# Attention and two gated layers on one core: the written order goes on through three units of the second block, with two places for values

## The chip, the cores and the metric

One core of one Trainium2 chip runs the whole program. The metric is the device time of one execution in microseconds (us), as the median of several runs. PE is the matrix engine, ACT the scalar engine, DVE the vector engine, POOL the GpSimd engine and SP the engine whose queue issues the transfers between DRAM and SBUF here.

## The reference

```python
# attention: chunks of 32 queries see 8 memory keys, 16 keys to the left, the chunk, 8 to the right
scores = scale * np.matmul(q_c, k_full.transpose(0, 1, 3, 2))
scores = scores - np.max(scores, axis=-1, keepdims=True)
a = np.exp(scores)
a = a / (np.sum(a, axis=-1, keepdims=True) + 1e-09)
out[:, :, c_start:c_end] = np.matmul(a, v_full)
...
x = out.transpose(0, 2, 1, 3).reshape(B * S, H * D)      # 3072 tokens x 512
h = x @ w_in                                             # 512 x 2048, float64
x = (h * (1.0 / (1.0 + np.exp(-1.702 * h)))) @ w_out     # 2048 x 512
g = x @ w_gate                                           # 512 x 1536
return (g * (1.0 / (1.0 + np.exp(-g))) * (x @ w_val) @ w_out2)
```

q, k and v are float32 of 4 batches, 8 heads, 768 positions, 64 wide; the weights of the layers come from the host as 64-bit floats. All arithmetic is done on the core.

## The kernel before

**Tiles.** The 3072 tokens are 24 *groups* of 128 (attention works on these) and 6 *blocks* of 512 (the layers work on these; block 0 is made of groups 0 to 3). The first layer has 8 *units* of 256 hidden columns. A unit of an ordinary block is a fast product: seven products of six matmuls of 256 columns (`product`, L430) into the banks `ps_a` and `ps_b`, with copies on ACT and additions on DVE between them, then curve, gate, cast and remainder for each half, then four *down chunks* of six matmuls (`down`, L558), one for each 128 output columns, which add up in the banks y0 to y3. Each operand of a product is held as a rounded part and a remainder, so a "split" is a cast on ACT and a subtraction on POOL or DVE.

**Token sums.** The seven operands of a block's products are made once for a block from its 128x4x512 tile `xf` (class `Tokens`, L381): `sum(k)` forms four differences, two of them in place in `xf`, `split_hi` and `split_lo` make the rounded parts and remainders.

**Weights.** A unit needs four tiles of 64-bit words (`raw`, 512 KB each, loaded by `load_raw`, L258; for the first layer those of the input weights come in two transfers of 64 partitions). A tile is turned into float32 by one ACT and two DVE instructions (L279, L287, L292), then POOL forms sums and the splits follow.

**Attention of a group.** Keys (`kbd`) and queries are loaded, `ps_s` gets the scores, DVE and ACT make the weights, four PE transposes turn them (`ps_t`), ACT copies them into `ebd`, the value product (`ps_o`, or `ps_v` in the opening) reads `ebd` and `vm`, ACT copies the result into `xf` and SP stores it to DRAM (`xd`). There is one place for values (`vm`) and two for turned weights (`ebd`).

**What sets the order.** Every engine executes in the order in which the program issues. The *opening* is written out by hand: the string `OPENING` (L796) is a list of names, and each name issues one step on its engine. It holds the attention of groups 0 to 7, the plain products of units 0 and 1 for block 0 (`plain_up`, L519; 48 matmuls of 512 columns), the first unit's down chunks, the weights of units 0 and 1, and the token sums of block 1. Behind it runs a loop (L865) over the blocks and units: it issues a unit (`unit`, L448), puts down chunks of earlier units between its products, takes one step of the next block's attention at fixed places (`PLACES`, L855), and lets `pace` (L820) make weights ahead. The first entries of the loop's list are block 0 with units 0 and 1 and blocks 1 to 5 with units 0 to 3. In the opening SP's transfers stand in the written order too.

Of the kernel before, what the change touches and what calls it, by code (L numbers as in the profile page):

```python
# [57 lines left out]
def tile_attention_moe_moe(  # L58
# [40 lines left out]
    vm = apool.tile([P, HP, 4, D], F32, name="vm")  # L99
    ebd = [apool.tile([P, HP, 4, 2, CH], F32, name=f"ebd{i}") for i in range(2)]  # L100
# [12 lines left out]
    def load_kv(n, g):  # L113
        if n == "v":
            nc.sync.dma_start(out=vm, in_=vg[g])
# [42 lines left out]

    def keep_e(g, ps, engs):
        for e, copy in enumerate(engs):  # L160
            r = slice(64 * e, 64 * e + 64)
            copy(ebd[g % 2][r, :, :, e, :], ps[r].rearrange("p a (c q) -> p a c q", c=4))  # L162

    def values(g, ps, v):
        ps = ps.rearrange("p (a q) -> p a q", a=KC)
        for a in range(0, HP, 2):
            for c in range(4):
                for j in range(2):
# [3 lines left out]
                        ebd[g % 2][:, a + j, c].rearrange("p e q -> p (e q)"),  # L172
# [17 lines left out]
    def st_scores(g):  # L190
        ps = bank("ps_s").rearrange("p (h k) -> p h k", h=H)
        q = qt.pop(g)
        for hp in range(HP):
            for c in range(4):
# [3 lines left out]
                )  # L198
        if g + 1 < NG:
# [74 lines left out]
    nraw, bits = [len(AT)], {}  # L274
# [80 lines left out]
    ready = {(1, u) for u in range(PLAIN)}  # L355

    def all_weights():
        for ph in (1, 2):
            for u in range(PLAIN if ph == 1 else 0, UNITS[ph]):
# [4 lines left out]
    need, made = [next(weights)], [20 * PLAIN]  # L364
# [16 lines left out]
    class Tokens:  # L381


        def __init__(self, src, engs):
            n = BLK // 2
            self.b11, self.b12 = src[:, 0:2, :n], src[:, 0:2, n:]
# [4 lines left out]
        def sum(self, k):  # L391
# [5 lines left out]
            elif k == 1:  # L397
                eng.tensor_sub(self.b12, self.b12, self.b11)
# [3 lines left out]
            else:  # L402
                eng.tensor_sub(self.b11, self.b21, self.t2)  # L403

# [153 lines left out]
    def down(ph, b, u, first, last, gs, base, dst, d, scale, passes=PASSES):  # L558
# [16 lines left out]
        if ends:  # L575
            del acc[d]
            if base is not None:
                t = base[d]
                nc.vector.scalar_tensor_tensor(t, y, scale, t, op0=ALU.mult, op1=ALU.add)
            else:  # L580
                t = opool.tile([P, 512], F32, tag="o", name="o")
                if d % 2 == 0:
                    nc.scalar.activation(t, y, AF.Copy, scale=scale)
                else:
                    nc.vector.tensor_scalar_mul(t, y, scale)
# [388 lines left out]
```

## Time and profile before

| | us |
|---|---|
| median of 3 runs | 1205.7 |
| lowest and highest | 1204.4, 1206.23 |
| the profiled execution | 1204.81 |
| its span | 1203.0 |
| PE busy | 1155.2 (96%) |
| DVE, ACT, POOL busy | 649.2, 566.7, 352.5 |

The span runs from the first to the last instruction that the profiler records; the profiled execution's own time is 1.8 us longer. Busy times of different engines lie beside each other, so they do not add up. A busy PE may still run at a lower clock, which a line of the page shows by the slice.

### The profile page before, as it was taken

What the parts mean: (1) busy time and instruction counts of PE and PEld (TensorE: products, weight loads), DVE (VectorE), ACT (ScalarE), POOL (GpSimd) and SP (SyncE); (2) the same over time, 40 slices, a digit from 0 to 9 for tenths busy, and PEclk for the clock granted to TensorE, in tenths of its full rate; (3) what the DMA queues carried; (4) which work ended last, traced back from release to release, by engine and by line L of the source; (5) the groups of instructions that cost most, each with busy time, mean ns of one, the idle gap of its engine ahead of it and who ended that gap; (6) DMA issues with size and microseconds to landing.
All of it is one profiled execution on the core that took longest, in us unless ns stands there. A gap on an engine that the chain in (4) does not pass through costs nothing.

```text
span 1203.0 us, 22302 instructions
## 1 busy us (share of the span) xinstructions
PE 1155.2 (96%) x8908; PEld 1042.7 (87%) x8908; DVE 649.2 (54%) x1117; ACT 566.7 (47%) x1185; POOL 352.5 (29%) x321
## 2 busy tenths in 40 slices
PE   4868899999999999999999999999999999999998
PEld 3757788888889999898998989999998989999997
DVE  6666665575674444443456564444556454454553
ACT  4655555454565544543465553342455443343342
POOL 2653312020455331320245433120255521020110
PEclk9888999999999999999999999999999999999999
DMA  9957363633434324223222331110225120320302
GB/s 309 301 161 196 120 177 104 170 106 114 141 123 124 105 89 140 85 74 106 96 97 88 123 123 36 71 55 17 88 76 168 56 97 10 106 80 27 106 23 84
DMA packets 62920, 131.47 MB, mean 109 GB/s; under 512 B 5728, under 2 KB 26208, under 8 KB 60512
## 3 DMA queue, kind: packets, MB, share of 16 engines
q1 hardware_dynamic: 62816, 130.05, 34.5%
q8 instruction: 70, 1.15, 0.4%
q14 instruction: 34, 0.28, 0.1%
HBM read 98.57 MB, written 31.46 MB: 108 GB/s over the span
## 4 chain that ended last, share of the span: by engine, by line
PE 85%; DMA 4%; DVE 4%; ACT 3%; issue 2%; POOL 1%; SPq 0%; DVEq 0%; ACTq 0%; POOLq 0%
PE y L568 35%; PE ps_a L433 26%; PE ps_c L433 12%; PE ps_b L433 8%; DMA raw<-in_wr 1%; DMA vm<-in_vg 1%; PE ps_o L169 1%; PE ps_s L196 1%; PE ps_u L529 1%; DMA xd<-xf 1%; DMA w<-in_kg 1%; PE ps_t L156 1%; ACT ebd L162 0%; DVE gs L548 0%; DVE b L419 0%
## 5 line engine op out<-in xcount | busy, mean ns | idle before, releaser
L433 PEld LDWEIGHTS ps_a<-b,w 128*128 128x128 f32 x2832 | 385.3, 190 | 50.6 <-ACT p L466 11.4
L433 PE MATMUL ps_a<-b,w 128*128 128x256 f32 x2832 | 398.6, 283 | 16.2 <-ACT p L466 10.1
L568 PE MATMUL y<-gs,w 128*128 128x512 f32 x1152 | 300.4, 396 | 1.0 <-DVE gs L548 0.8
L568 PE MATMUL y<-w,gs 128*128 128x512 f32 x864 | 247.8, 395 | 0.6 <-DVE gs L548 0.5
L568 PEld LDWEIGHTS y<-gs,w 128*128 128x128 f32 x1152 | 204.6, 190 | 37.1 <-DVE gs L548 2.3
L433 PE MATMUL ps_c<-b,w 128*128 128x256 f32 x1224 | 179.1, 282 | 0.0
L433 PEld LDWEIGHTS ps_c<-b,w 128*128 128x128 f32 x1224 | 167.1, 190 | 8.8
L568 PEld LDWEIGHTS y<-w,gs 128*128 128x128 f32 x864 | 144.2, 190 | 14.5 <-DVE gs L548 1.7
L249 POOL TENSOR_TENSOR w<-wf,w 128x512 fp32r<-128x512 f32 (+1 forms) x68 | 78.0, 1148 | 227.3 <-ACT w L246 215.2
L433 PE MATMUL ps_b<-b,w 128*128 128x256 f32 x900 | 135.4, 287 | 1.0 <-DVE e L131 0.5
L433 PEld LDWEIGHTS ps_b<-b,w 128*128 128x128 f32 x900 | 120.7, 193 | 5.8 <-issue 2.1
L536 ACT ACTIVATE g<-ps_b 128x512 f32<-128x512 f32 x72 | 43.0, 598 | 166.0 <-DVE ps_b L491 166.0
L419 DVE TENSOR_TENSOR b<-xl,b 128x512 fp32r<-128x512 f32 x72 | 64.5, 895 | 80.5 <-ACT b L415 80.3
L485 DVE TENSOR_TENSOR ps_a<-m,ps_a 128x256 f32<-128x256 f32 x118 | 50.2, 425 | 105.4 <-PE ps_a L433 99.4
L475 ACT COPY u<-ps_a 128x256 f32<-128x256 f32 x118 | 44.0, 373 | 109.1 <-PE ps_a L433 108.8
L403 POOL TENSOR_TENSOR xl<-xl,t 128x512 f32<-128x512 f32 x18 | 23.3, 1293 | 231.0 <-DVE t L401 229.8
L548 DVE TENSOR_TENSOR gs<-ps_a,gs 128x512 fp32r<-128x512 f32 x118 | 80.9, 686 | 10.4 <-ACT gs L544 10.1
L470 DVE TENSOR_TENSOR ps_b<-p,ps_b 128x256 f32<-128x256 f32 x118 | 50.4, 427 | 60.6 <-PE ps_b L433 55.2
L544 ACT CAST gs<-ps_a 128x512 fp32r<-128x512 f32 x118 | 69.8, 591 | 25.1 <-DVE ps_a L514 15.7
L514 DVE TENSOR_TENSOR ps_a<-g,ps_a 128x512 f32<-128x512 f32 x72 | 50.0, 694 | 46.0 <-PE ps_a L433 45.5
L466 ACT COPY p<-ps_a 128x256 f32<-128x256 f32 x118 | 44.0, 373 | 58.4 <-PE ps_a L433 54.2
L491 DVE TENSOR_TENSOR ps_b<-u,ps_c 128x256 f32<-128x256 f32 x102 | 43.6, 427 | 50.0 <-PE ps_c L433 49.7
(112 smaller groups left out, 1182.4 us busy)
## 6 DMA issues: line engine op xcount, KB each, us to landing
raw<-in_wr SPq DMA_DIRECT2D x49, 512.0 KB, 3.4
xl<-yd SPq DMA_DIRECT2D x12, 1024.0 KB, 4.8
vm<-in_vg SPq DMA_DIRECT2D x19, 512.0 KB, 4.1
kbd<-in_kg SPq DMA_DIRECT2D x32, 256.0 KB, 4.1
raw<-in_wr SPq DMA_DIRECT2D x30, 256.0 KB, 4.2
yp<-o SPq DMA_DIRECT2D x24, 256.0 KB, 3.0
xl<-xd SPq DMA_DIRECT2D x6, 1024.0 KB, 4.8
base<-yp SPq DMA_DIRECT2D x24, 256.0 KB, 3.6
```

Source lines behind the costliest of these rows:

```text
L249: nc.gpsimd.tensor_sub(w[:, 1, o : o + n], f, w[:, 0, o : o + n].bitcast(F32))
L419: self.engs[k].tensor_sub(x[:, 1], self.source(k), x[:, 0].bitcast(F32))
L433: nc.tensor.matmul(ps, w[:, a, o + kc * P : o + kc * P + P], x[:, c, kc, :], start=(start and kc == 0 and (a, c) == PASSES[0]), stop=(kc = ...
L466: nc.scalar.copy(p1, ca[:, :n])
L470: add(cb[:, :n], p1, cb[:, :n])
L475: nc.scalar.copy(u2, ca[:, :n])
L485: add(ca[:, n:], m, ca[:, :n])
L491: add(cb[:, n:], u2, cc)
L514: late[0] = [lambda: nc.vector.tensor_mul(ca, t, ca), lambda: gs.append(cast(ca))]
L544: nc.scalar.copy(x[:, 0], g)
L548: nc.vector.tensor_sub(x[:, 1], g, x[:, 0].bitcast(F32))
L568: nc.tensor.matmul(y, lhs, rhs, start=(first and o == 0 and (a, c) == PASSES[0]), stop=(ends and o == len(gs) - 1 and (a, c) == passes[-1]),)
```

## The change

The opening goes on: the string now also holds units 0 to 2 of block 1 (products, curves, down chunks), the second unit's down chunks of block 0 with their evictions and stores, the attention of groups 8 to 11 (block 2), and the weights of units 2 and 3. The loop then skips these: for block 1 it issues no unit before unit 3 and no attention. All of the opening's steps stand in a new order. The reciprocal becomes a step apart from the weighing. `vm` becomes two tiles, and in the loop the load for group g + 2 is issued behind the product of g; of the two `ebd` tiles one remains, the second is in the opening a borrowed weight slot. Two of block 1's token sums go to tiles of their own (`place`) in place of `xf`.

```diff
-    vm = apool.tile([P, HP, 4, D], F32, name="vm")
-    ebd = [apool.tile([P, HP, 4, 2, CH], F32, name=f"ebd{i}") for i in range(2)]
+    vm = [apool.tile([P, HP, 4, D], F32, name=f"vm{i}") for i in range(2)]
+    ebd = [apool.tile([P, HP, 4, 2, CH], F32, name="ebd")]
...
     def st_pv(g):
-        ps = values(g, bank("ps_o"), vm)
-        if g + 1 < NG:
-            load_kv("v", g + 1)
+        ps = values(g, bank("ps_o"), vm[g % 2])
+        if g + 2 < NG:
+            load_kv("v", g + 2)
...
-    ready = {(1, u) for u in range(PLAIN)}
+    ready = {(1, u) for u in range(2 * PLAIN)}
...
-    need, made = [next(weights)], [20 * PLAIN]
+    need, made = [next(weights)], [40 * PLAIN]
...
             elif k == 1:
-                eng.tensor_sub(self.b12, self.b12, self.b11)
+                b12, self.b12 = self.b12, self.place(self.b12)
+                eng.tensor_sub(self.b12, b12, self.b11)
...
             else:
+                self.b11 = self.place(self.b11)
                 eng.tensor_sub(self.b11, self.b21, self.t2)
+
+        def place(self, t):
+            if not self.apart:
+                return t
+            return opool.tile([P, BLK], F32, tag="o", name="t").rearrange("p (k n) -> p k n", k=2)
...
+    def unit_product(new, out, w, o, k):
+        def f(u):
+            if new:
+                un[u][new] = bank(f"ps_{new}")
+            key, off = ((1, u, w), o) if w != "v" else ((1, u - u % 2, "v"), u % 2 * HALF)
+            product(out(u), wt[key], off, tokens().ops[k], start=out is cb1 and k == 2 or new is not None)
+
+        return f
...
     OPENING = """
-        z0 tb0 z1 ldk0 ldq0 ldk1 ldq1 ldq2 ldk2 ldk3 ldw0 ldq3 ldw1 sc0 ldv0 mx0 ldq4 sc1 ldv1 ldk4 ex0 mx1 z2
...
+        z0 tb0 z1 ldk0 ldq0 ldq1 ldw0 ldq2 ldk1 ldk2 ldk3 sc0 ldv0 ldq3 mx0 ldq4 ex0 ldw1 pr0 sm0 cs0 sc1 ldv1
...
+        qe2 cm2 ct14 qf2 ya1 ac2 wo6 ldw17 ad2 wol6 ct15 ka2 qg2 kb2 wo7 ldw18 yb1 ma2 wol7 kc2 yc1
     """
...
-            places = PLACES[u - ua] if n and attends else ()
+            places = PLACES[u - ua] if n > 1 and attends else ()
...
-            if n:
+            if n == 1 and u < 3:
+                gs = seconds[u]
+            elif n:
                 gs = unit(ph, u, ops, chunk, after, n < NBLK - 1, ph == 1 and ua > 0, nxt is None and last)
```

The matrix engine, where the first unit of block 1 begins. `ps_t` is a turn, `ps_v` a value product, `ps_s` are scores of a group from 8 on, `y_...` are down chunks of block 0, `ps_a` and `ps_b` the unit's products. Before, from the turn of group 7:

```order
L156 MATMUL ps_t<-ident,e 128x128 x4
L568 MATMUL y_910<-gs,w 128x512 x6
L156 MATMUL ps_t<-ident,e 128x128 x4
L169 MATMUL ps_v<-ebd_119,w 64x2x32 x16
L169 MATMUL ps_v<-ebd_118,vm 64x2x32 x16
L433 MATMUL ps_a<-b,w 128x256 x6
L433 MATMUL ps_b<-b,w 128x256 x6
L433 MATMUL ps_a<-b,w 128x256 x6
L196 MATMUL ps_s<-kbd,q 32x128 x16
L433 MATMUL ps_b<-b,w 128x256 x6
L568 MATMUL y_851<-gs,w 128x512 x6
```

The same place now, from a down chunk and the values of group 7:

```order
L585 MATMUL y_973<-gs,w 128x512 x6
L174 MATMUL ps_v<-w,vm_118 64x2x32 x16
L201 MATMUL ps_s<-kbd,q 32x128 x16
L158 MATMUL ps_t<-ident,e 128x128 x4
L585 MATMUL y_973<-gs,w 128x512 x6
L585 MATMUL y_1067<-gs,w 128x512 x6
L174 MATMUL ps_v<-ebd,vm_117 64x2x32 x16
L450 MATMUL ps_a<-b,w 128x256 x6
L585 MATMUL y_922<-gs,w 128x512 x6
L450 MATMUL ps_a<-b,w 128x256 x6
L450 MATMUL ps_b<-b,w 128x256 x6
L450 MATMUL ps_a<-b,w 128x256 x6
```

Scores of group 9, a turn, two down chunks and the values of group 8 now stand between the values of group 7 and the first product of the unit; before, only the values of group 6 stood there.

The vector engine at the token sums of block 1 (`t<-xf` and `xf<-xf,t` are sums, `b<-...` remainders of the operands). Before:

```order
L292 SCALAR_TENSOR_TENSOR wf<-raw,wf 128x512
L292 SCALAR_TENSOR_TENSOR wf<-w,wf 128x512
L396 TENSOR_TENSOR t_977<-xf 128x512
L401 TENSOR_TENSOR t_983<-t_977,xf 128x512
L403 TENSOR_TENSOR xf<-xf,t_983 128x2x256
L419 TENSOR_TENSOR b<-t_983,b 128x512
L419 TENSOR_TENSOR b<-t_977,b 128x512
L419 TENSOR_TENSOR b<-xf,b 128x512
L470 TENSOR_TENSOR ps_b<-p_1005,ps_b 128x256
```

Now:

```order
L412 TENSOR_TENSOR t_1056<-t_1037,xf 128x512
L125 TENSOR_REDUCE m<-ps_s 128x8
L131 TENSOR_TENSOR e<-ps_s,m 128x512
L609 TENSOR_SCALAR o<-y_973 128x512
L436 TENSOR_TENSOR b<-t_1056,b 128x512
L415 TENSOR_TENSOR t<-xf,t_1056 128x512
L296 TENSOR_SCALAR wf<-wh 128x512
L143 TENSOR_REDUCE r<-e 128x8
L436 TENSOR_TENSOR b<-t_1037,b 128x512
L301 SCALAR_TENSOR_TENSOR wf<-raw,wf 128x512
L821 TENSOR_TENSOR ps_b<-p_1126,ps_b 128x256
L436 TENSOR_TENSOR b<-t,b 128x512
```

The last difference goes to a tile `t` of its own in place of `xf`, and the attention of group 9, an eviction and words of a weight tile now stand between the remainders, which stood in one row.

The queue of SP from the second plain unit's end on (`vm` are values, `xd` the stores of attention results, `yp` those of block 0's output). Before:

```order
L267 DMA raw<-in_wr 128x512
L188 DMA xd_90<-xf 512x1x128 x2
L115 DMA vm<-in_vg 128x1024
L119 DMA kbd<-in_kg 64x1024 x2
L110 DMA q<-in_qg 128x512
L267 DMA raw<-in_wr 128x512
L586 DMA yp_101<-o 128x512 x2
```

Now:

```order
L115 DMA vm_117<-in_vg 128x1024
L276 DMA raw<-in_wr 128x512
L115 DMA vm_118<-in_vg 128x1024
L193 DMA xd_90<-xf 512x1x128
L672 DMA q<-in_qg 128x512
L119 DMA kbd<-in_kg 64x1024 x2
L193 DMA xd_90<-xf 512x1x128
L794 DMA yp_101<-o 128x512
L115 DMA vm_117<-in_vg 128x1024
L794 DMA yp_101<-o 128x512
L119 DMA kbd<-in_kg 64x1024 x2
L193 DMA xd_91<-xf 512x1x128
```

Values of two groups now stand ahead of the last stores of block 1's tokens (`xd_90`), and a second weight tile between them.

## Rows read from the trace of the kernel before

**Rows 1.** The page: the granted clock of PE in 40 slices, in tenths.

```profile
PEclk9888999999999999999999999999999999999999
```

**Rows 2.** Busy time by stretch: PE, PEld, DVE, ACT, POOL, then clock, DMA share, GB/s.

```profile
38.80:130.30 91.50, 73.05 (x737) 60.62 (x737) 57.12 (x93) 53.66 (x107) 43.40 (x40) 0.91 0.74 216
130.30:1203.00 1072.70, 1062.63 (x7575) 965.54 (x7574) 568.08 (x980) 493.93 (x1037) 293.43 (x258) 1.00 0.29 93
...
38.80:62.30 23.50, 23.32 (x274) 18.88 (x273) 16.35 (x28) 18.51 (x37) 14.55 (x14) 1.00 0.94 297
...
70.80:84.50 13.70, 13.06 (x116) 10.60 (x116) 10.64 (x16) 4.60 (x10) 7.89 (x9) 0.81 0.42 136
```

**Rows 3.** The chain of waits: start, duration, what; pieces of PE.

```profile
129.26 2.22 PE ps_a L433 x12
...
39.10 6.83 PE ps_u L529 x30
...
137.50 0.72 PE ps_a L433 x6
138.21 1.39 PE y L568 x6
...
145.95 1.01 PE ps_s L196 x32
...
159.59 1.08 PE ps_o L169 x32
```

**Rows 4.** Waits of PE from 62 to 131 us, then from 130 us on.

```profile
PE ps_a L433 <- ACT p L466: 9.3, 2, 6.8
PE ps_a L433 <- ACT ebd L162: 3.8, 1, 3.8
PE ps_o L169 <- DMA vm<-in_vg: 2.7, 1, 2.7
...
PE y L568 <- DVE gs L548: 1.3, 3, 0.8
```

**Rows 5.** The chain of waits from 63 to 75 us.

```profile
63.14 3.53 DMA xd<-xf
66.83 1.27 POOL xf L398
68.12 1.67 ACT b L415 x3
...
71.47 3.44 DVE b L419 x2
```

**Rows 6.** The timeline of PE: a turn, and the scores of group 7.

```profile
153.30 0.60 PE L156 MATMUL ps_t<-ident,e 128*128 128x128 f32 x4
...
49.88 0.86 PE L677 MATMUL ps_k<-w,qq 64*32 64x64 f32 x64
```

**Rows 7.** The chain of waits at the fourth values.

```profile
23.72 10.51 DMA vm<-in_vg
...
37.81 0.91 issue
```

**Rows 8.** Busy time by stretch, columns as in rows 2.

```profile
0.00:30.00 30.00, 14.11 (x472) 11.70 (x473) 18.80 (x34) 14.65 (x31) 8.81 (x17) 1.00 0.98 309
30.00:60.00 30.00, 26.63 (x338) 21.78 (x339) 20.28 (x38) 20.81 (x45) 21.08 (x21) 0.89 1.01 301
...
84.50:106.00 21.50, 17.17 (x172) 14.83 (x172) 15.31 (x27) 13.71 (x28) 8.11 (x8) 0.92 0.84 221
```

**Rows 9.** The timeline at the token sums: DVE alone, DVE beside POOL.

```profile
63.07 0.69 DVE L396 TENSOR_TENSOR t<-xf 128x512 f32<-128x512 f32 x1 [1.80 <-ACT xf L183]
73.15 1.76 DVE L419 TENSOR_TENSOR b<-xf,b 128x512 fp32r<-128x512 f32 x1
...
72.64 1.72 POOL L249 TENSOR_TENSOR w<-w 128x512 fp32r<-128x512 f32 x1
```

**Rows 10.** The timeline of PE: a down chunk behind a pause.

```profile
91.22 2.35 PE L568 MATMUL y<-gs,w 128*128 128x512 f32 x6
```

More of the change, by code (lines that the diff above doesn't have):

```diff
@@ L198, in st_scores @@
                 )
+        return ps
+    def st_scores(g):
+        ps = scores(g)
         if g + 1 < NG:
@@ L556, in tile_attention_moe_moe, with down @@
     acc = {}
-    def down(ph, b, u, first, last, gs, base, dst, d, scale, passes=PASSES):
+    def down(ph, b, u, first, last, gs, base, dst, d, scale, passes=PASSES, held=None):
         if d not in acc:
@@ L574, in down, with evict @@
                 )
[L575 to L585, printed above, removed]
-            nc.sync.dma_start(out=dst(b, d), in_=t)
+        if not ends:
+            return
+        del acc[d]
+        if held is not None:
+            held[d] = y
+            return
+        nc.sync.dma_start(out=dst(b, d), in_=evict(y, base, d, scale))
+    def evict(y, base, d, scale):
+        if base is not None:
+            t = base[d]
+            nc.vector.scalar_tensor_tensor(t, y, scale, t, op0=ALU.mult, op1=ALU.add)
+            return t
+        t = opool.tile([P, 512], F32, tag="o", name="o")
+        if d % 2 == 0:
+            nc.scalar.activation(t, y, AF.Copy, scale=scale)
+        else:
+            nc.vector.tensor_scalar_mul(t, y, scale)
+        return t
     def entries(ph, ends):
@@ L741, in down_first, with down_second, evict_first, store_first @@
         down(1, 0, 0, True, False, firsts[0], None, None, d, 0.5)
+    def down_second(d):
+        down(1, 0, 1, False, True, firsts[1], None, None, d, 0.5, held=full)
+    full = {}
+    def evict_first(d):
+        full[d] = evict(full[d], None, d, 0.5)
+    def store_first(d):
+        nc.sync.dma_start(out=yp[0][:, d, :], in_=full.pop(d))
+    seconds, un = [[] for _ in range(3)], [{} for _ in range(3)]
+    QN = BLK // 2
+    def quarter(bank_, part):
+        return lambda u: un[u][bank_][:, part * QN : part * QN + QN]
+    ca0, ca1, cb0, cb1 = quarter("a", 0), quarter("a", 1), quarter("b", 0), quarter("b", 1)
+    def unit_product(new, out, w, o, k):
[5 more added lines that the diff above has]
+        return f
+    def unit_copy(name, src):
+        def f(u):
+            un[u][name] = cpool.tile([P, QN], F32, tag=name, name=name)
+            nc.scalar.copy(un[u][name], src(u))
+        return f
+    def unit_add(out, name, src):
+        return lambda u: V.tensor_add(out(u), un[u][name], src(u))
+    def unit_curve(bank_):
+        return lambda u: un[u].update({"t" + bank_: curve(un[u][bank_], 1)})
+    def unit_gate(bank_):
+        return lambda u: gate(un[u][bank_], un[u].pop("t" + bank_), un[u][bank_])
+    def unit_cast(bank_):
+        return lambda u: seconds[u].append(cast(un[u][bank_]))
+    def unit_rest(bank_):
+        return lambda u: rest(un[u][bank_], seconds[u]["ab".index(bank_) ^ 1])
+    def unit_down(d):
+        return lambda u: down(1, 1, u, u == 0, False, seconds[u], None, None, d, 0.5)
     def tokens():
         if not tok:
-            tok.append(Tokens(xf[1], [G, G, G, V, G, V, V, V, G, V, V]))
+            tok.append(Tokens(xf[1], [G, G, G, V, G, V, V, V, G, V, V], True))
         return tok[0]
@@ L810, in tile_attention_moe_moe @@
     tok = tok[0]
-    for i in range(SPARE):
-        give_w(("spare", i))
+    late[0] = [lambda: unit_rest("b")(2), lambda: unit_gate("a")(2)]
+    late[1] = [lambda: unit_cast("a")(2)]
+    late[2] = [lambda: unit_rest("a")(2)]
     open_ctx.close()
@@ L918, in tile_attention_moe_moe @@
             done += 1
-        if not n:
-            pends[0] = None
         if n == NBLK - 2:
```

126 lines of the change are left out of this document (91 added, 35 removed).

## The prediction

> **What bounds the kernel now.** First the page: the granted clock stands below 0.9 only near the start [rows 1]. Then busy time by stretch, cut at two places in the program [rows 2]: 38.8 us, where the first plain product starts, and 130.3 us, where unit 3 of block 1 starts, the first unit that both versions leave to the general loop (half of the twelve matmuls at 129.26 us are its own, [rows 3]). Behind 130.3 us the PE is busy 1062.6 of 1072.7 us at full clock: nothing to win there. Between the cuts it is busy 73.05 of 91.5 us at clock 0.91. I call this stretch the stage; it holds the second half of what was written by hand and all that the change newly writes by hand.
>
> What ends the idle time of the stage is in the PE's waits [rows 4]: 9.3 us for a copy of ACT, 3.8 us for another, 2.7 us for values. The chain of waits says why the longest, 6.8 us, is there [rows 5]: unit 0 of block 1 needs its token sums; one is written in place into the tile that is just being stored, so POOL sits until the store has landed (3.53 us), and ACT's casts and DVE's remainders follow one by one to 74.9 us.
>
> **The change, part by part.** Work neither goes away nor comes; it changes places. *What the stage costs the PE if it never waits*, by pieces at full clock [rows 3, 6]: 48 plain matmuls at 6.83/30 us, 10.9; 7 turns at 0.60, 4.2; 8 value products at 1.08, 8.6; 4 scores at 1.01, 4.0; 15 down chunks at 1.39, 20.9; 21 unit products at 0.72, 15.1. Sum 63.7 us, against 91.5 now. So 27.8 us is the most to win here: 18.5 us of idle time, 9 of matmuls at reduced clock. That all of it could go depends on the other engines: in the same 91.5 us DVE is busy 57.1, ACT 53.7, POOL 43.4 and the DMA engines 0.74 x 91.5 = 68 [rows 2]. None but DMA passes 63.7, and DMA can be let out partly: stores, and loads for later units, aren't needed by the end of the stage.
>
> *Start.* The new order puts input tile 2 (512 KB) ahead of the fourth values. In the trace that load takes 10.51 us from issue to landing and everything up to 34.3 us waits for it [rows 7], at 300 GB/s with the DMA engines full [rows 8]: 0.524 MB / 0.305 = 1.7 us later. Scores of group 7 (0.86 us) come in front of the first plain product, a turn (0.60) goes behind it [rows 6], and 0.91 us in which the PE now waits for nothing there [rows 7] may cover part: 1.05 to 1.96 us. I take 1.4: start at 40.2 us, and without any wait the stage would end at 103.9.
>
> *Token sums.* Two results now go to tiles of their own, so nobody waits for the store: the 6.8 us go. The PE rows show cover that wasn't there: between values of group 7 and the first unit product stand scores, a turn, two down chunks and values (5.5 us) where now only group 6's values stand. What is late next is the chain itself: xf copy, POOL difference, cast, POOL remainder. From [rows 5] twice 1.27 on POOL and 0.56 for a cast, with the copy about 4 us: covered by 5.5. Cost 0 to 2 us; I take 1, since DVE and POOL slow each other in just this spot (below).
>
> *The wait that takes its place.* There is one input tile for tokens, and the copy of group 8 into it has to wait for the stores of groups 4 to 7. The last of these stands behind 22.5 MB in SP's written order (k and v 512 KB each, q, xd and yp 256, weight tiles 512, by their shapes). At 0.305 MB/us it lands at 73.8 us. ACT reaches that copy behind the copy of unit 0's m, which needs the fifth product: 40.2 + 31.3 (8 plain parts, 4 turns, 5 values, 2 scores, 5 chunks, 5 unit products) = 71.5 us. So ACT stands 2.3 us, and behind it the casts of unit 2's weights and the two curves of unit 0; on the PE the turn of group 9 waits for the bank that this copy empties. Scores of group 10 wait for their keys (22.3 MB, 73.1 us) at the same place, so the two do not add up. Bounds 0 (stores overtake) and 7 us (a landing of 10.51 us as in a full queue [rows 7] instead of the 3.53 waited for now [rows 5]); I take 3, near the sum.
>
> *Banks.* Scores of group 11 need the bank that unit 0's second half frees after curve, gate, cast and remainder, four steps of 0.56 to 0.69 us [rows 5, 9] on two engines; three down chunks (4.2 us) lie over it. 0 to 2 us, taken 0.5.
>
> *Values.* With two places the load of group g + 2 leaves at the product of g. This takes the 2.7 us wait [rows 4]; behind 130.3 us no wait for values is among the PE's, so nothing more. The last values of the stage stand behind 26.7 MB: 87.5 us, while the PE asks for them at about 92. One place for turned weights costs nothing in the loop: the copy for group g + 1 is issued behind the product that reads g.
>
> *Weights.* Tiles for units 2 and 3 are loaded and split in the written part, not by the pacing loop: same instructions, same count. The loading in two transfers of 64 partitions is the same code in both: nothing.
>
> *Small waits.* From 38.8 to 62.3 us [rows 2], where the PE already follows a written order, pieces of 22.8 us took 23.5: 3%. Of 63.7 us that is 1.9.
>
> Sum: 103.9 + 3 + 1 + 0.5 + 1.9 = 110.3 us for the end of the stage, 20.0 earlier. The block's next sums gain too: the stores that they wait for are over two units earlier, so 0.8 us of PE wait behind 130.3 [rows 4] goes. 1204.8 (the profiled execution; span 1203.0) - 20.8 = 1184.0; the median of the runs is 0.9 above the profiled one: **1185 us**.
>
> **A rule against it.** DVE's remainder with two SBUF operands took 1.76 us beside a POOL subtraction (1.72), where alone such an instruction takes 0.69 [rows 9]. The Trainium skill, "SBUF — State Buffer", section "SBUF: two separate sides", states that GpSimd and a DVE instruction with two SBUF inputs take an exclusive lock on a shared port pair, and the loser waits for the whole instruction. By that rule the order, which packs both engines closer, pays more; the row agrees, and the price is the third rival's.
>
> **Rivals.**
> 1. *No wait at all*: 104 to 105 us, 26 us won and 0.8: 1179. For it: the 23.5 us that already run at 3%. Against: four engines and DMA would be over 80% busy at once.
> 2. *DMA sets the pace.* From 84.5 to 106 us the engines of DMA were 0.84 busy at only 221 GB/s [rows 8]: half tiles and stores move less. At 40.2 us some 12.3 MB are through; the other 14.4 to the last values take 65 us at 221: 105.4. Behind them stand 1.1 us of values, 14 unit products and 3 chunks (14.2): 120.7. Won 9.6 + 0.8: 1195.
> 3. *DVE against POOL.* 26 DVE instructions with two SBUF operands lie in the stage (7 weighings, 13 joins, 3 sums, 3 remainders). With POOL busy 43.4 of 70 us, 0.62 x 26 x 1.07 us = 17 us, on top of the 57.1 that DVE is busy today: 74 us, end at 114.5 or, with the store wait, 117. Won 13.3 + 0.8: 1192.
> 4. *Slower: the PE falls to the lower clock.* Behind a pause of the PE the granted clock falls towards the lower of its two levels, 1.2 GHz: one down chunk took 2.35 us [rows 10], where its pieces sum to 1.39 at full clock; from 70.8 to 84.5 us the granted clock was 0.81 though the PE was busy 13.06 of 13.7 us [rows 2]. If the new order trades few long waits for many short ones, as much idle time (18.5 us) at clock 0.81 throughout gives 63.7 / 0.81 + 18.5 = 97.1: end at 137.3, 7 us lost, 1213. It decides from 90.1 us on, that is with 18.5 us of waits from a mean clock below 0.89. Against: the waits have named causes, and those are taken away.
> 5. *Given back*: units behind the stage start earlier but wait for weights or stores. Behind 130.3 us DMA is 0.29 and POOL 27% busy [rows 2], so I give this little; it would end near 1204.
>
> **How the numbers follow.** Forecast (1180 to 1190) 0.50, no wait 0.12, DMA 0.14, DVE and POOL 0.11, slower 0.08, given back 0.05. 1177 to 1198 leaves out the last two and some of the first two rivals, about 0.18. A measurement here tells 0.2%, 2.4 us, from no change: faster by more 0.87, same 0.05, slower 0.08.
>
> **What would show it.** In the new profile unit 3 of block 1 should start near 110 us and the first plain product near 40. The wait before the first product of unit 0 should be under 2 us. ACT should wait some 3 us for a store at the copy of group 8. PE waits in the stage should sum to under 9 us and the granted clock there be above 0.95; DMA should be over 0.85 busy from 40 to 90 us. Wrong, if unit 3 starts behind 120 us, if the longest wait is for keys or values (rival 2), if remainders of 1.7 us are the rule (3), or if the clock of the stage is below 0.9 (4). If the stage is right and the time isn't, the loop behind it has changed.

## The result

The changed kernel takes 1190.7 us (1188.7 to 1191.2), the kernel before 1206.0 beside it: a ratio of 0.9872 with a 95% interval of 0.9855 to 0.9889, so some 15 us faster. 1185 was predicted, with 1177 to 1198 as the range. The side and the range were right; of 20.8 us expected, 15.2 came. The numbers below are of the profiled execution, 1190.33 us with a span of 1188.6.

The page of the changed kernel, its span, the busy time of the engines and the granted clock in 40 slices [rows 1]:

```profile
span 1188.6 us, 22301 instructions
...
PE 1151.3 (97%) x8908; PEld 1039.6 (87%) x8908; DVE 652.1 (55%) x1117; ACT 568.1 (48%) x1185; POOL 354.9 (30%) x321
...
PEclk9889999999999999999999999999999999999999
```

The engines do what they did before; the time lies in the order. The first plain product now starts at 42.1 us and unit 3 of block 1 at 116.4, so the stage is the stretch between. Busy time by stretch, changed kernel, columns as in [rows 2]; the first three lines cut the span at those two places, the others are pieces of the stage:

```profile
0.00:42.10 42.10, 20.51 (x661) 16.82 (x661) 25.25 (x48) 22.26 (x48) 18.24 (x27) 0.84 1.01 310
42.10:116.40 74.30, 68.60 (x683) 57.55 (x678) 59.09 (x89) 51.44 (x102) 43.01 (x38) 0.95 0.86 258
116.40:1188.60 1072.20, 1062.21 (x7573) 965.24 (x7571) 567.78 (x981) 494.43 (x1036) 293.61 (x258) 1.00 0.29 93
...
60.00:78.40 18.40, 14.65 (x181) 11.72 (x180) 17.56 (x20) 12.95 (x26) 15.72 (x13) 0.97 0.90 315
...
66.00:80.00 14.00, 10.88 (x82) 8.71 (x81) 13.19 (x16) 7.86 (x17) 12.50 (x10) 0.91 0.74 257
...
78.40:85.00 6.60, 6.58 (x55) 5.88 (x56) 3.33 (x7) 2.49 (x5) 2.72 (x3) 0.56 0.23 60
```

Against [rows 2], the stage went from 91.5 to 74.3 us, the stretch behind it from 1072.7 to 1072.2. What precedes the stage grew from 38.8 to 42.1. So 17.2 us were won in the stage and 0.5 behind it, and 3.3 were lost ahead of it.

Of the 74.3 us, the PE's pieces at full clock are 63.7 (the prediction's own sum). Idle time is 74.3 - 68.6 = 5.7 us, and 3.75 of it lies between 60 and 78.4 us. From 78.4 to 85 us the PE is busy all the time at a clock of 0.56, close to the lower of its two levels (1.2 GHz): (1 - 0.56) x 6.6 = 2.9 us. The remaining 2.0 us are small.

The waits of PE from 38 to 130 us in the changed kernel (who waited, for whom: total, times, longest), to be held against [rows 4]:

```profile
PE ps_a L450 <- ACT p L816: 1.2, 1, 1.2
PE ps_k L706 <- issue: 1.2, 1, 1.2
PE ps_b L450 <- DVE ps_b L821: 1.2, 1, 1.2
PE ps_a L450 <- DVE b L436: 1.0, 1, 1.0
...
PE ps_b L450 <- POOL b L436: 0.5, 1, 0.5
PE ps_a L450 <- POOL b L436: 0.3, 1, 0.3
```

The waits of 6.8, 3.8 and 2.7 us are gone, and no wait for values is among the new ones. What is left is short. Three of these lines are remainders of the token sums (`b`, L436), a fourth the addition that DVE does behind them (L821): 3.0 us together. The timeline of DVE there shows why, against [rows 9]:

```profile
73.16 1.49 DVE L296 TENSOR_SCALAR wf<-wh 128x512 int32<-128x512 int32 x1 [0.63 <-POOL raw L327]
...
75.17 1.17 DVE L436 TENSOR_TENSOR b<-t,b 128x512 fp32r<-128x512 f32 x1
76.26 1.76 DVE L301 SCALAR_TENSOR_TENSOR wf<-raw,wf 128x512 int32<-128x512 int32 x1
77.95 0.42 DVE L821 TENSOR_TENSOR ps_b<-p,ps_b 128x256 f32<-128x256 f32 x1
```

A shift (L296) and a join (L301) of a weight tile that is needed much later stand between the remainders, and beside POOL they take 1.49 and 1.76 us. The PE stands behind the addition at 77.95. The timeline of PE in the changed kernel, the same place:

```profile
76.39 0.85 PE L450 MATMUL ps_a<-b,w 128*128 128x256 f32 x5 [1.00 <-DVE b L436]
78.42 1.65 PE L450 MATMUL ps_b<-b,w 128*128 128x256 f32 x6 [1.17 <-DVE ps_b L821]
80.00 1.94 PE L201 MATMUL ps_s<-kbd,q 128*32 128x128 f32 x32
81.87 1.65 PE L450 MATMUL ps_b<-b,w 128*128 128x256 f32 x6
```

Behind four short pauses (0.31, 0.45, 1.00 and 1.17 us within 8 us) six matmuls take 1.65 us, where in the same timeline six took 0.88 at 72.98 us, and scores take 1.94 where they took 1.08 at 64.51 us. The hypothesis for the experiments was therefore: the missing 6 us lie at the token sums (a DVE too full beside POOL, and the low clock behind it) and ahead of the stage.

### The profile page after: what moved, and what is told of

Its sections match the earlier page's. It is cut to its first block, busy times and chain, and to the rows that moved or that the text cites. A ratio compares the mean times of both kernels' runs of the same rounds, so it can differ in the third digit from the quotient of the medians.

```text
span 1188.6 us, 22301 instructions
## 1 busy us (share of the span) xinstructions
PE 1151.3 (97%) x8908; PEld 1039.6 (87%) x8908; DVE 652.1 (55%) x1117; ACT 568.1 (48%) x1185; POOL 354.9 (30%) x321
## 3 DMA queue, kind: packets, MB, share of 16 engines
q8 instruction: 70, 1.15, 0.4%
## 4 chain that ended last, share of the span: by engine, by line
PE 86%; DMA 5%; DVE 3%; ACT 2%; issue 2%; POOL 1%; SPq 0%; DVEq 0%; ACTq 0%; POOLq 0%
PE y L585 35%; PE ps_a L450 27%; PE ps_c L450 12%; PE ps_b L450 9%; DMA raw<-in_wr 2%; PE ps_s L201 1%; PE ps_o L174 1%; DMA q<-in_qg 1%; DMA w<-in_kg 1%; DMA xd<-xf 1%; PE ps_t L158 1%; PE ps_v L174 1%; ACT ebd L167 0%; PE ps_u L546 0%; ACT g L551 0%
## 5 line engine op out<-in xcount | busy, mean ns | idle before, releaser
L436 DVE TENSOR_TENSOR b<-xl,b 128x512 fp32r<-128x512 f32 x72 | 64.3, 893 | 80.4 <-ACT b L432 80.3
```

Of the source, the lines that this page charges most:

```text
L436: self.engs[k].tensor_sub(x[:, 1], self.source(k), x[:, 0].bitcast(F32))
```

## The experiments

All ratios are against the kernel before, run on the same chip. In the order's names, `pr`, `cs` and `ct` are the three steps on the words of a weight tile (ACT L288, DVE L296, DVE L301), `sumA` and `sumB` sums of weights on POOL, `sc`, `mx`, `ex`, `sm` scores, exponents and sums of a group, `tl` and `ts` remainders and sums of tokens, `ldw` and `ldv` loads of weight tiles and values, `wg` the weighing.

### Which part of the change brings the gain

**The place alone.** The kernel before, with the two token sums in tiles of their own.

```diff
-            tok.append(Tokens(xf[1], [G, G, G, V, G, V, V, V, G, V, V]))
+            tok.append(Tokens(xf[1], [G, G, G, V, G, V, V, V, G, V, V], True))
```

> The kernel before with one part of the change: two token sums go to tiles of their own. Theory A (the 6.8 us wait of the PE comes from the store): POOL's 3.6 us wait goes, the PE's longest wait falls to about 3 us, time 4 to 5 us less than before, 1201. Theory B (the chain of casts and remainders is long enough by itself, with DVE and POOL in each other's way): under 2 us less.

1201.5 us, ratio 0.9967 (0.9954 to 0.998): 3.8 us faster. POOL's wait for the store, 3.53 us in [rows 5], is gone. The wait of 6.8 us in [rows 4] isn't; the timeline of PE in this kernel at the first product of unit 0 shows what is left of it:

```profile
69.44 1.78 PE L441 MATMUL ps_a<-b,w 128*128 128x256 f32 x6 [4.47 <-ACT p L474]
```

The casts and remainders that follow one another still take 4.47 us in an order in which the PE has nothing else to do.

**Place and values, in the old order.** The same, and two tiles for values with one for turned weights.

```diff
-    vm = apool.tile([P, HP, 4, D], F32, name="vm")
-    ebd = [apool.tile([P, HP, 4, 2, CH], F32, name=f"ebd{i}") for i in range(2)]
+    vm = [apool.tile([P, HP, 4, D], F32, name=f"vm{i}") for i in range(2)]
+    ebd = [apool.tile([P, HP, 4, 2, CH], F32, name="ebd")]
...
-        ts0 st6 ldv8 hiA1 ts2 ts1 ts3 tc3 wol2 tl3 tc2 tc5 tl2 tl5 tc4 tc6 tl4 tl6 loA1
+        ts0 st6 ldv8 ldv9 hiA1 ts2 ts1 ts3 tc3 wol2 tl3 tc2 tc5 tl2 tl5 tc4 tc6 tl4 tl6 loA1
```

> The kernel before with two parts of the change, all but the order: token sums in tiles of their own, two places for values with the load two groups ahead and one place for turned weights in the loop. If the parts add up (4 to 5 us of the sums, 2.7 us of the wait for values and the 0.8 us of low clock behind it): 7 to 8 us less than before, 1198; the written order then is worth the other 7. If the wait for values is only handed on to the next step (weights, DVE): 4 to 5 us less, 1201.

1202.6 us, ratio 0.9976 (0.9966 to 0.9987): no more than the place alone. The wait for values is gone (0.4 us is left at the value product, for a copy of ACT), yet behind it the block's next token sums wait for a store. The chain of waits of this kernel:

```profile
128.39 5.36 DMA xd<-xf
...
133.94 0.69 DVE xf L403
134.63 0.61 DVE gs L559
...
135.29 0.74 PE y L579 x2
```

The values come earlier, and the time is handed on to the next thing that was late. This kernel also gives up a place for turned weights: the PE's wait for a copy into `ebd` is 4.1 us here and 3.2 in the kernel with the place alone, so the second place for values by itself was not tested in the old order. So the written order brings the larger part of the 15 us, about 11, if the place is worth the same in it.

**The place taken away from the new order.** Two kernels have the token sums in place again. In the first, the store of group 6 stands behind the difference that overwrites the tile, so that this part of the output holds changed values:

```diff
-            tok.append(Tokens(xf[1], [G, G, G, V, G, V, V, V, G, V, V], True))
+            tok.append(Tokens(xf[1], [G, G, G, V, G, V, V, V, G, V, V]))
```

> The changed kernel, but the two token sums are written in place again, as before the change. Theory A (a tile of its own is worth the store's landing): POOL's difference, at 67.9 us now, waits for the last store of groups 4 to 7 (issued 68.1 us, about 4 us to landing), so every remainder behind it on POOL comes 4 us later: time 3 to 5 us more, 1194 to 1196. Theory B (the order hides it, since other POOL and DVE work stands between): within 1.5 us of 1190.

1192.0 us, ratio 0.989 (0.9872 to 0.9908), 1.3 us slower than the changed kernel by the medians, with intervals that overlap. Here the difference needn't wait for the last store, only for earlier ones; POOL still waits 5.19 us for them and the PE 4.0 us for POOL's remainder, and most of that is made up elsewhere. The second puts the difference behind the store in the order too:

```diff
-        xf6 sc9 xf7 ldv9 rs3 sumA2 tc0 st7 ts0 te8 ldq11 tc1 dm1 ldk10 ts2 ts1 ec8 mx9 st6 dn2 tl0 tc3 ev1 pr10
+        xf6 sc9 xf7 ldv9 rs3 sumA2 tc0 st7 ts0 te8 ldq11 tc1 dm1 ldk10 ts2 ec8 mx9 st6 ts1 dn2 tl0 tc3 ev1 pr10
```

> As the changed kernel with the two token sums in place, now with group 6's store ahead of the difference that overwrites it, so that POOL waits for all four stores. Theory A (in the first such kernel, where group 6's store came behind the difference, the PE waited 4.0 us more for POOL's first remainder): the wait is 4 to 6 us, time 3 to 6 us over the changed kernel, 1194 to 1196. Theory B (the stage gives part of any delay back, as DVE and POOL then meet less): about 2 us more, 1192.5.

1194.5 us, ratio 0.9908 (0.9895 to 0.9922), 3.8 us slower than the changed kernel by the medians. Now POOL sits out the whole store, and the PE with it. The timeline of POOL in this kernel:

```profile
76.39 1.26 POOL L409 TENSOR_TENSOR xf<-xf 128x512 f32<-128x512 f32 x1 [6.58 <-DMA xd<-xf]
```

And the longest of its PE's waits from 38 us on:

```profile
PE ps_a L450 <- POOL b L436: 6.3, 1, 6.3
```

Against the second of these kernels, which overwrites nothing that is still to be stored, the place is worth about 4 us in either order, though the wait that it takes away is nearly twice as long in the new one: part of 6.3 us is made up elsewhere.

**One place for values in the new order.** From group 8 on only one of the two tiles is used, and the load for g + 1 stands behind the product of g, in the loop and (not shown) in the string.

```diff
-        ps = values(g, bank("ps_o"), vm[g % 2])
-        if g + 2 < NG:
-            load_kv("v", g + 2)
+        ps = values(g, bank("ps_o"), vm[0])
+        if g + 1 < NG:
+            load_kv("v", g + 1)
...
-        at["x", g] = values(g, bank("ps_v"), vm[g % 2] if g >= 2 * GRP else v_open[g % 3])
+        at["x", g] = values(g, bank("ps_v"), vm[0] if g >= 2 * GRP else v_open[g % 3])
...
```

> The changed kernel with one place for values from group 8 on: each load leaves behind the product that frees it, in the opening and in the loop. Theory A (two places are needed only where the order is dense): values of groups 10 and 11 are waited for, 1 to 3 us each with some low clock behind, nothing in the loop: time 2 to 6 us more, 1193 to 1196. Theory B (SP's queue holds its transfers in any case): within 1 us.

1195.3 us, ratio 0.9907 (0.9884 to 0.993), 4.6 us slower than the changed kernel by the medians, with intervals that just touch. The timeline of PE in this kernel:

```profile
99.44 1.97 PE L174 MATMUL ps_v<-ebd,vm 128*64 128x64 f32 x32 [3.88 <-DMA vm<-in_vg]
101.34 2.93 PE L585 MATMUL y<-gs,w 128*128 128x512 f32 x6
```

The wait for values is back inside the stage, 3.88 us, and behind it a value product takes 1.97 us and a down chunk 2.93, where the timeline of the changed kernel has 1.15 (at 90.16 us) and 1.55 (at 71.59 us): the low clock makes it dearer. In the loop behind the stage no wait for values appears. The new order needs the second place; in the old one it gave nothing measurable together with the place for turned weights that it cost.

### Where the missing 6 us are

**Words and sums of weights taken out of the token sums.** Sums of unit 2's weights and the words of tiles 10 and 11 go behind the remainders.

```diff
-        xf6 sc9 xf7 ldv9 rs3 sumA2 tc0 st7 ts0 te8 ldq11 tc1 dm1 ldk10 ts2 ts1 ec8 mx9 st6 dn2 tl0 tc3 ev1 pr10
-        pv8 tl3 tc2 sy1 sumB2 ex9 qa0 ts3 ldv10 tc5 dm0 tl1 cs10 cp0 sm9 tc4 qc0 tl5 tl2 ev0 qb0 cu0 ct10 sy0
-        tc6 qe0 tl4 ab0 ra9 qd0 pr11 tl6 wv2 sc10 rc9 cm0 wvl2 wg9 xf8 qf0 ldk11 ac0 hiA2 te9 ad0 hiB2 loA2 qg0
+        xf6 sc9 xf7 ldv9 rs3 tc0 st7 ts0 te8 ldq11 tc1 dm1 ldk10 ts2 ts1 ec8 mx9 st6 dn2 tl0 tc3 ev1 pv8 tl3 tc2
+        sy1 ex9 qa0 ts3 ldv10 tc5 dm0 tl1 cp0 sm9 tc4 qc0 tl5 tl2 ev0 qb0 cu0 sy0 tc6 qe0 ab0 tl4 ra9 qd0 tl6
+        sumA2 wv2 sc10 rc9 cm0 sumB2 pr10 cs10 ct10 pr11 wvl2 wg9 xf8 qf0 ldk11 ac0 hiA2 te9 ad0 hiB2 loA2 qg0
```

> The changed kernel, but POOL's two pairs of weight sums of unit 2 and DVE's two instructions for weight tile 10 stand behind the last remainder of block 1's token sums instead of among them. Theory A (DVE and POOL hold each other up there: joins of 1.67 to 1.76 us, DVE busy 13.2 of 14.0 us from 66 to 80 us): the PE's waits of 0.45, 1.00 and 1.17 us between 73 and 78 us go and the clock of 80 to 90 us rises from 0.79 to 1.00; unit 3 of block 1 starts 4 to 6 us earlier, time about 1186. Theory B (DMA sets the pace, 0.86 busy in the stage): the same steps are late for their data, unit 3 starts within 1 us of 116.4 and the time stays near 1190.

1189.7 us, ratio 0.9875 (0.9855 to 0.9895): no measurable gain. The remainders are in time, with one wait of 0.5 us left. But the weighing of group 9 (`wg9`) now stood behind the words, and these wait for POOL. The waits of PE in this kernel from 38 us on, the longest:

```profile
PE ps_t L158 <- DVE e L153: 3.1, 1, 3.1
```

The granted clock from 80 to 90 us is low again, at 0.83, behind that one wait. The gain did not come, but the cause was only moved a few instructions on, so the question stays open for the next kernel.

**The same, with the words behind the weighing** (called the cleared order below). `pr10` goes behind `ac0`, `cs10` and `ct10` behind `ad0`, `pr11` behind `mc0`:

```diff
-        sumA2 wv2 sc10 rc9 cm0 sumB2 pr10 cs10 ct10 pr11 wvl2 wg9 xf8 qf0 ldk11 ac0 hiA2 te9 ad0 hiB2 loA2 qg0
-        st8 mx10 ka0 ldq12 dn3 ma0 loB2 kb0 ex10 dm2 mb0 kc0 ldw12 sm10 mc0 dm3 md0 ldw13 ra10 ec9 rc10 sc11 kd0
+        sumA2 wv2 sc10 rc9 cm0 sumB2 wvl2 wg9 xf8 qf0 ldk11 ac0 pr10 hiA2 te9 ad0 cs10 ct10 hiB2 loA2 qg0 st8
+        mx10 ka0 ldq12 dn3 ma0 loB2 kb0 ex10 dm2 mb0 kc0 ldw12 sm10 mc0 pr11 dm3 md0 ldw13 ra10 ec9 rc10 sc11
```

> As the first clearing of the token sums, but DVE's two instructions for weight tile 10 stand behind the weighing of group 9 and the additions of unit 0, so that nothing on the path waits for POOL's sums. Theory A (first clearing: token waits of the PE fell from 2.9 to 0.5 us, and 3.1 us came back because the weighing stood behind words that waited 1.9 us for POOL): the 3.1 us wait goes and the clock stays at 1.00 until 100 us; unit 3 of block 1 starts near 111, time 3 to 5 us under the changed kernel: 1186. Theory B (any step taken out of there is paid a little later, since DVE and POOL have no slack in the whole stage): within 1.5 us of 1190.

1186.3 us, ratio 0.9834 (0.9814 to 0.9854), 4.5 us faster than the changed kernel by the medians, with intervals that do not meet. Busy time by stretch in this kernel, columns as in [rows 2]:

```profile
66.00:80.00 14.00, 13.48 (x143) 11.63 (x136) 12.82 (x19) 10.38 (x22) 12.80 (x11) 1.00 0.84 280
80.00:90.00 10.00, 8.50 (x95) 6.88 (x94) 9.14 (x15) 7.36 (x15) 3.65 (x3) 1.00 1.05 248
```

Where the changed kernel had the PE busy 10.88 of 14 us at 0.91, it is now busy 13.48 at 1.00, and the clock stays at 1.00 behind it. Unit 3 starts at 112.25 us, 4.2 earlier, though the first plain product starts 0.8 later. DVE is as full as before (12.82 of 14 us beside 12.80 of POOL); what changed is whose work comes first. That holds of POOL too, whose sums of unit 2's weights were moved with the words: its last remainder for block 1 starts at 73.11 us instead of 75.75. How much of the gain is DVE's order and how much POOL's was not separated. The hypothesis on the token sums holds, and this version beats both kernels.

**The words of tile 15 behind the copy of unit 2's p.** In the changed kernel ACT takes these words ahead of a curve and of that copy, and their load is late. The chain of waits of the changed kernel there, which ends in the PE's wait of 1.2 us for p:

```profile
98.19 8.16 DMA raw<-in_wr
...
106.43 0.10 ACT wh L288
...
107.00 1.07 ACT g L551 x2
108.07 0.27 ACT p L816
...
108.38 0.98 PE ps_a L450 x6
```

```diff
-        ac1 loB3 qg1 ad1 pr15 cs14 ka1 qa2 cs15 loA3 ldw16 ma1 kb1 qb2 cp2 mb1 kc1 qc2 ab2 mc1 qd2 kd1 cu2 md1
+        ac1 loB3 qg1 ad1 cs14 ka1 qa2 loA3 ldw16 ma1 kb1 qb2 cp2 pr15 mb1 cs15 kc1 qc2 ab2 mc1 qd2 kd1 cu2 md1
```

> The changed kernel, but ACT takes the words of weight tile 15 (and DVE shifts them) behind the copy that unit 2's second product waits for. Theory A (at 106.4 us ACT stands 2.06 us for that tile, and the curves of unit 1 and the copy stand behind it): the PE's 1.2 us wait goes, time 1 to 1.5 us less, 1189.5. Theory B (curves and copy are late anyway): under 0.5 us.

1188.9 us, ratio 0.9857 (0.9835 to 0.9879). The wait is gone, and from the first plain product to unit 3 the PE needs 73.0 us instead of 74.3. The 1.8 us between the medians is inside the uncertainty, and the 1.3 us of the stage aren't the wait's alone: this profile lost 1.5 us to the low clock from 70 to 94 us where the changed kernel's lost 2.9. Put together with the cleared order (the words behind the weighing):

> The second clearing of the token sums together with the words of tile 15 behind unit 2's first copy. Theory A (the clearing took the low clock and the wait for that copy with it: there is no such wait in its profile): nothing added, 1186 within 1 us. Theory B (ACT's stand of 2 us for tile 15 still costs something later in units 1 and 2): 1 us less, 1185.

1186.4 us, ratio 0.9834 (0.9821 to 0.9848): nothing on top of the cleared order, among whose waits no such line is left.

**Input tile 2 behind the fourth values.** This tests the term of 1.7 us in the prediction's start.

```diff
-        pr1 ldw2 te1 mx3 ra2 pv0 ldk5 ec1 rc2 cs1 ldk6 ex3 ct1 ldk7 pv1 hi0 wg2 sumA0 ldv3 wv0 sm3 wb0 xf0 wbl0
+        pr1 te1 mx3 ra2 pv0 ldk5 ec1 rc2 cs1 ldk6 ex3 ct1 ldk7 pv1 hi0 wg2 sumA0 ldv3 ldw2 wv0 sm3 wb0 xf0 wbl0
```

> The changed kernel, but weight tile 2 is loaded behind the fourth values instead of ahead of them. Theory A (the first plain product starts late, 42.1 against 38.8 us, because 512 KB more stand ahead of those values): they land 1.7 us earlier, the plain products start near 40.4, time 1.5 to 2 us less, 1189. Theory B (the start is set by scores of group 7 and by pauses in which the PE waits for nothing shown): no change, or the sums of the first unit's weights come later: within 0.7 us.

1189.3 us, ratio 0.9864 (0.9841 to 0.9886): the same within the uncertainty, and the first plain product started later, at 43.34. The values were issued 2.1 us earlier, but now ACT stands at the words of tile 2, and the copy that the fourth value product needs is queued behind them. The timeline of ACT in this kernel, then that of PE:

```profile
34.73 0.66 ACT L288 ACTIVATE wh<-raw 128x512 f32<-128x512 f32 x1 [7.53 <-DMA raw<-in_wr]
```

```profile
39.27 1.98 PE L174 MATMUL ps_v<-w,vm 128*64 128x64 f32 x32 [4.96 <-ACT w L167]
```

The values landed at 32.5 us here (issued at 22.35, 10.1 us to landing), earlier as the prediction's term has it. But ACT takes the words of tile 2 ahead of that copy, and as long as it does, the order of the two loads is worth nothing. An order in which ACT too takes them later was not run.

This kernel shows something else. At the token sums its PE has the same four pauses as the changed kernel (0.30, 0.46, 0.99 and 1.17 us), and yet the clock does not fall behind them. The timeline of PE at the last of them, then the stretch from 80 to 90 us (columns as in [rows 2]), which stood at 0.79 in the changed kernel:

```profile
79.95 0.97 PE L450 MATMUL ps_b<-b,w 128*128 128x256 f32 x6 [1.17 <-DVE ps_b L821]
```

```profile
80.00:90.00 10.00, 10.00 (x136) 8.47 (x136) 8.73 (x16) 7.22 (x14) 3.67 (x4) 1.00 0.72 180
```

Three more profiles have these four pauses (the words of tile 15, scores of group 7, one place for values). From 70 to 94 us they lost 1.5 us each to the lower clock, the changed kernel's lost 2.9, and this one nothing. So what the clock takes behind the same pauses differs from profile to profile.

**Scores of group 7 behind the first plain products.** The PE starts the stage after these, and pauses inside them. The timeline of PE in the changed kernel:

```profile
36.90 1.97 PE L174 MATMUL ps_v<-w,vm 128*64 128x64 f32 x32 [1.28 <-ACT e L134]
...
41.34 0.83 PE L706 MATMUL ps_k<-w,qq 64*32 64x64 f32 x62 [1.19 <-issue]
42.10 1.66 PE L546 MATMUL ps_u<-xh,w 128*128 128x512 f32 x6
```

```diff
-        sm5 ex6 sc7 hi3 sm6 ldq8 pr3 xl3 ra6 ra5 ldv5 pr4 cs3 ec4 rc5 ua0 ct3 ldv6 mx7 ldq9 sumA1 wb1 ua1 wv1
-        pr5 st1 rc6 ex7 wg5 sumB1 ub0 hiA1 wg6 st2 xf3 loA1 ub1 cs4 hiB1 sm7 th0 ct4 wvl1 te5 st3 ra7 th1 ua2
+        sm5 ex6 hi3 sm6 ldq8 pr3 xl3 ra6 ra5 ldv5 pr4 cs3 ec4 rc5 ua0 ct3 ldv6 ldq9 sumA1 wb1 ua1 sc7 wv1 pr5
+        st1 rc6 wg5 sumB1 ub0 hiA1 wg6 mx7 st2 xf3 loA1 ub1 cs4 hiB1 ex7 th0 ct4 sm7 wvl1 te5 st3 ra7 th1 ua2
```

> The changed kernel, but scores of group 7 (and their DVE and ACT steps) stand behind the first two plain parts instead of in front of the first. Theory A (in eight profiles with the new order the first plain product started at 41.7 to 44.3 us, against 38.5 to 40.0 with the old one, because these scores and the pause of 1.2 to 2.2 us within them stand ahead): it starts 2 to 3 us earlier, near 40, and the time falls by 1.5 to 2.5 us, to 1188.5. Theory B (the pause belongs to the PE's place in time, not to the scores: it then stands within the plain products): under 1 us gained, 1190.

1188.2 us, ratio 0.9857 (0.9844 to 0.9871), 2.5 us faster than the changed kernel by the medians, with intervals that overlap. The first plain product starts at 38.77 instead of 42.10, unit 3 at 114.56 instead of 116.38: of 3.3 us, 1.8 reach the end of the stage. The scores (0.86 us) and what is left of the pause now lie inside the stage; beside them this profile has a new wait of 1.0 us for values and lost 1.5 us less to the low clock, so the balance is rough. (Seven profiles of the new order had started the stage at 41.7 to 44.3, one of them, with tile 2 moved, without a pause there.) The pause of 1.19 us is 0.37 in this kernel:

```profile
38.77 1.63 PE L546 MATMUL ps_u<-xh,w 128*128 128x512 f32 x3
40.77 0.86 PE L546 MATMUL ps_u<-xh,w 128*128 128x512 f32 x3 [0.37 <-issue]
```

It now stands in the plain products, as theory B has it: in both kernels it lies behind the 598th or 599th matmul of the program, and what the edit moved is what stands there.

**All of it.** The token sums cleared, the words of tile 15 and the scores of group 7 moved.

> The second clearing of the token sums, the words of tile 15 moved, and scores of group 7 behind the first two plain parts. Theory A (the start and the token sums are two separate places on the path): the gains add, 4.5 and 1.8 us under the changed kernel: 1184.5, unit 3 of block 1 starts near 110.5. Theory B (what starts earlier waits at the token sums, where DVE and POOL have no slack left): as the clearing alone, 1186.3.

1185.8 us, ratio 0.9834 (0.9817 to 0.9851): the stage starts at 38.68 and unit 3 at 111.55, but the time is that of the cleared order alone (1186.3, with 42.88 and 112.25). Of a lead of 4.2 us, 0.7 reach the end. Where it goes is in the waits of PE from 38 to 70 us in this kernel:

```profile
PE ps_u L546 <- issue: 1.4, 1, 1.4
PE ps_v L174 <- DMA w<-in_vg: 0.7, 1, 0.7
PE ps_v L174 <- DMA vm<-in_vg: 0.6, 1, 0.6
PE ps_t L158 <- ACT xf L188: 0.5, 1, 0.5
```

The scores (0.86 us) and the pause (1.36) lie inside the stage now; two waits for values and one for a copy of ACT take another 1.8. Together that is 4.0. The values of group 7 start at 63.79 us here and at 64.04 in the cleared order: the lead is gone before the token sums begin. Of these 4.0 us, 1.3 are a PE that asks earlier for values that have not landed; the scores and the pause only changed sides. The cleared order alone is as good as everything together.

## Why the prediction was right, and where it was off

- **Where the time was to come from** was right: out of the stage, with the stretch behind it as good as unchanged. The three named waits went. Behind the stage 0.5 us were gained where 0.8 were predicted, but not by the wait that was named: the PE's listed waits there sum to 5.6 us, where they were 5.5, and 0.4 of the 0.5 is busy time (1062.6 to 1062.2).
- **The start** was mis-sized: 42.1 us instead of 40.2, so 3.3 us of delay where 1.4 was taken. The transfer's term of 1.7 us was right in size: the fourth values landed at 34.23 us before [rows 7], and at 35.87 to 36.23 us in three profiles with the new order of loads (the cleared order, scores of group 7, all together). In the changed kernel's profile the value product starts 2.5 us later (36.90 against 34.36), since a step of ACT came last there. The step that failed is the pause that "may cover part": it covered nothing, and came on top of the scores behind the product. With the scores moved, the start was back at 38.77, 0.8 of the 3.3 us because the value product itself came earlier in that profile.
- **Token sums** were the largest miss: 1 us taken, 0 to 2 as bounds. The changed kernel has 3.0 us of waits there and 2.9 us of low clock behind them, and clearing the place won 4.5 us. The step that failed is the cover of "5.5 us" for "the chain itself": it counted the PE work ahead of the first product, but not what the new order puts between the remainders on DVE. The third rival had the right mechanism at the wrong size. It added 17 us to DVE's 57.1, but these held stretched instructions already (three remainders at 1.76 us and one sum at 1.74, where 0.69 is the time alone [rows 9]); in the changed kernel's stage DVE is busy 59.1 us, not 74. What counts is the place: the clearing won 4.5 us in 14 us of the stage. The joins of weight words show the stretching; first the nine in the changed kernel's stage, then the eleven in the stage of before, by line and form (busy time, mean ns of one):

```profile
L301 DVE SCALAR_TENSOR_TENSOR wf<-raw,wf 128x512 int32<-128x512 int32 x9 | 10.0, 1113 | 0.1
```

```profile
L292 DVE SCALAR_TENSOR_TENSOR wf<-raw,wf 128x512 int32<-128x512 int32 x11 | 7.5, 686 | 0.1
```

The mean rose from 0.69 to 1.11 us: five of the nine took 0.68 or 0.69 us with POOL idle, four 1.51 to 1.76 beside POOL. The Trainium skill, "SBUF — State Buffer", section "SBUF: two separate sides", lets a DVE instruction with two SBUF inputs and a GpSimd instruction exclude each other for a whole instruction. These rows agree.
- **The lower clock**, the fourth rival, came true at one spot only: 2.9 us at 78.4 to 85 us. The sum had no term for it. In the changed kernel's profile it stands behind a row of short pauses, as the rival said, and it went with them in the cleared order. But the pauses alone don't settle it: behind the same four the clock took between nothing (tile 2 moved) and 2.9 us, so a wait at that place costs itself and up to as much again. What decides is open. (The rival's 2.35 us beside 1.39 are two measures: in the timeline a chunk at full clock takes 1.55 us.)
- **The store wait** of 3 us was wrong: it is 0. The transfer was not quicker than worked out: the last of these stores was issued at 68.1 us and landed at most 7.9 us later, so by 76 where 73.8 was expected. It was ACT that came later, at 80.4 us instead of 71.5, because the copy of m ahead of it needs the fifth product, which ended only near 80 us (ACT waited 3.78 us for it). In the cleared order that copy stands at 76.9, still without a wait. The bound of 0 was the right one, and here luck helped the total: 3 us that never came made up for more than half of what the token sums cost beyond their term. The timeline of ACT in the changed kernel:

```profile
80.11 0.37 ACT L816 COPY m<-ps_b 128x256 f32<-128x256 f32 x1 [3.78 <-PE ps_b L450]
80.38 0.59 ACT L188 COPY xf<-ps_v 128x512 f32<-128x512 f32 x1
```

- **DMA** was 0.88 busy from 40 to 90 us, as foretold, and did not set the pace: no wait for keys or values of the PE lies in the stage of the changed kernel, so the second rival didn't happen. Its price took 221 GB/s from a stretch with the DMA engines 0.84 busy; the changed stage moved 258 at 0.86. It stands close, though: with all moves together the PE waited for values twice. **Values** were right for the new order. The **small waits** (1.9 us) and the **banks** (0.5) were taken too low: 2.7 us of idle time that isn't the token sums' (1.2 of it for p) and the 2.0 that no row names make 4.7. The first rival's counter, "over 80% busy at once", doesn't hold for POOL: 43.4 us of 64 are 0.68.

By terms the stage was to take 70.1 us and took 74.3: 3 us less for the store, 4.9 more for the token sums with the clock behind them, 2.3 more of small ones. With 1.9 at the start and 0.3 behind the stage this is, but for rounding, the 6.3 us between the 20.8 expected and the 14.5 that the two profiled executions differ by.

## What to carry to other kernels

When a written order removes long waits, look at what it now puts between the steps of the next dependent chain on the engines that were not the bound: work that is needed later (here weight words) ran in front of remainders that the matrix engine was waiting for, and moving a few names gave 4.5 us more. A second buffer is worth what the order makes of it: two places for values, taken with one place less for turned weights, gave nothing in the old order, and going back to one cost 4.6 us in the new one, where the load was needed earlier. And a wait priced from the chain alone can be too cheap, as the clock may fall behind it: here by nothing to 2.9 us behind the same four pauses.

## What the runs showed of the hardware

- Several short pauses of the matrix engine (0.31 to 1.17 us, 2.9 us together within 8 us) were followed by 6.6 us at a granted clock of 0.56 although the engine was then busy all the time. Behind the same pauses in the kernel with tile 2 moved the clock stayed at 1.00. In the cleared order, with a single pause of 0.5 us at that place, it stayed at 1.00; in the kernel ahead of it, with one of 0.5 and one of 3.1 us, it was 0.83 from 80 to 90 us.
- Beside POOL not only DVE's instructions with two SBUF operands are stretched. Of the twelve shifts with one operand in the changed kernel's stage, the five that began while a POOL instruction was running took 0.64 to 1.51 us, and four of them ended 0.28 or 0.29 us behind its end (the one at 73.16 us at 74.65, POOL's at 74.37; for the fifth the timeline doesn't give that end). Two that began just ahead of one (61.22 ahead of 61.44, 63.85 ahead of 64.06) took 0.41, and the five with POOL idle 0.41 to 0.43.
- Sixteen DMA engines busy 0.86 of 74 us, at 258 GB/s, did not bound the stage, but left little: with the earlier start the PE began to wait for values again.
- In 13 of the 14 profiles the matrix engine paused 0.37 to 3.42 us near 40 us, inside a row of turns, scores or plain products, while the waits name nothing ("issue"). The place is always behind the 598th or 599th matmul of the program, in the old order too. The trace does show something there. The page has a queue of its own for instructions (packets, MB, share of 16 engines):

```profile
q8 instruction: 70, 1.15, 0.4%
```

In all 13 the pause ends 1.2 to 1.5 us behind the end of one of these packets (in the changed kernel the packet ends at 39.92 us, the pause at 41.34). A like pause behind the 472nd or 473rd matmul ends 1.4 to 1.8 us behind an earlier packet, in all 14. With tile 2 moved the packet ended at 38.66 us, while the PE was still waiting for its value product (39.27), and there was no pause near 40 us. So the engine seems to wait for its own program there, in a stretch in which data keeps the DMA engines full (1.01 busy up to 42.1 us); no kernel was run that moves that transfer alone.
